# Linear attention feeding a gated two-layer network: joint token tails, loads held back and a second queue at the start

## The chip, the cores and the metric

The kernel runs on one core of a Trainium2 chip. The metric is device time in microseconds (us), the median of several executions; a trace of one execution per kernel gives the details, and its span is about 1.75 us shorter than the device time. The kernel before takes 296.5 us.

## The reference, cut to what matters

```python
# attention without softmax, 8 batches x 8 heads x 576 tokens x 64
q_p, k_p = phi(q), phi(k)               # phi(x) = min(exp(x), max(x, 0) + 1)
kv  = einsum('bhsd,bhse->bhde', k_p, v)
z   = sum(k_p, axis=2)
num = einsum('bhsd,bhde->bhse', q_p, kv)
den = einsum('bhsd,bhd->bhs', q_p, z) + 1e-6
x   = (num / den)                       # as [8*576 tokens, 512]
h   = x @ w_in                          # 512 -> 2048
g   = h / (1 + exp(-beta * h))
out = g @ w_out                         # 2048 -> 512
```

The 576 tokens of a batch are four tiles of 128 and a tail of 64. The eight tails are collected in `xT_tail` and go through the network last, as a ninth batch.

## The kernel before

The program is ordered by hand. Each batch has an input phase (`h_phase`, 64 matmuls of 512 columns and their silu on ScalarE, ACT) and an output phase (`y_phase`, 64 matmuls). The attention of the next batch is woven into them through `plan`: what to run after which matmul group. The parts that the change and the argument touch, with cuts marked `# ...`:

```python
def num_mm(b, t):                       # numerator and denominator of one token tile
    n = rows(t)                         # 128, or 64 for the tail
    # ...
    for p in range(KC):
        nc.tensor.matmul(nps[:n, p // 2, c0 : c0 + 2 * (D + 1)],
                         st[b, "qT"][:, t, p, :n], kv_bd[b % 2][p // 2][:, p % 2], ...)

# start: q, k, v and the weights all on GpSimd's queue; q, k, v and w_in are cast to bf16 on the way
load_nine(k9, k); load_nine(q9, q, j1=4); # ... v, rest of q, w_in, w_out, k and q of batch 1

# output phase of batch 0
load_next(2)                            # k, q, v of batch 2, behind v of batch 1 and the last of w_out
# ...
w_out_scale(2); phi(1, 1); v_copy(1); phi(1, 0)
y_phase_wide(0, {
    4: [F(load_next, 3)],
    9: [F(kv_mm, 1), F(kv_evac, 1), F(w_out_scale, 3)],
    10: [F(q_trans, 1, 0, 1, wide=True), F(q_trans, 1, 2, 3, wide=True)],
    11: [F(num_mm, 1, 0), F(num_norm, 1, 0)],
    # ...
})
# input phase of batch 1:  12: [F(v_copy, 2), F(load_next, 4)]
# output phase of batch 1: 1: [F(phi, 2, 0), F(q_trans_dma, 2), F(phi, 2, 1)]  (q of batch 2, by DMA)
```

Of the kernel before, what the change touches and what calls it, by code (L numbers as in the profile page):

```python
# [11 lines left out]
ALU = mybir.AluOpType  # L12
# [4 lines left out]
def kernel(  # L17
# [99 lines left out]
    def nine(a, spec):  # L117

        names = " ".join(spec)
        flat = a.rearrange("p a b c -> p (a b c)")  # L120
        size = {"h": HH, "j": N9, "d": D}
        n = size["h"] * size["j"] * size["d"]
        return flat[:, 0:n].rearrange(f"p ({names}) -> p {names}", **size)

    q9 = nine(xqk[0][:, 0], "hjd")
    k9 = nine(xqk[0][:, 1], "hjd")
    v9 = nine(vraw[0], "hjd")

    def load_nine(dst, src, h0=0, h1=HH, j0=0, j1=N9):
        for g in range(2):  # L130
            nc.gpsimd.dma_start(  # L131
                out=dst[g * TAIL : (g + 1) * TAIL, h0:h1, j0:j1, :].rearrange(
                    "p h j d -> p h (j d)"
                ),
                in_=src[0, g * HH + h0 : g * HH + h1, :, :]
                .rearrange("h (p j) d -> p h j d", j=N9)[:, :, j0:j1, :]
                .rearrange("p h j d -> p h (j d)"),
            )
# [4 lines left out]
    nc.vector.memset(g_sb[0][:, FC - 1, :], 0.0)  # L143
    clear_tail(1)
    nc.vector.memset(vraw[1][TAIL:P, :, NJ, :], 0.0)
    beta_row = consts.tile([FC, P], F32)
    nc.sync.dma_start(out=beta_row, in_=moe_beta.rearrange("(c p) -> c p", p=P))
# [3 lines left out]
    load_nine(k9, k)  # L151
    load_nine(q9, q, j1=4)
    make_identity(nc, identity)
    make_identity(nc, ident16)
    load_nine(v9, v, j1=6)
    load_nine(v9, v, j0=6)
    load_nine(q9, q, j0=4)
    for i in range(4):
# [9 lines left out]
    kv_bd = [  # L168
        [consts.tile([P, 2, 2, D + 1], BF16, name=f"kv_bd{i}{g}") for g in range(2)]
        for i in range(2)  # L170
    ]
    for i in range(2):
        for g in range(2):
            nc.vector.memset(kv_bd[i][g], 0.0)
# [32 lines left out]
    def w_out_scale(i, dve=True):  # L207
        for c in range(4):
            ff = 4 * i + c
            dst, src, by = w_out_sb[i][:, c, :], w_out_f[i][c // 2][:, c % 2, :], rbeta[:, ff : ff + 1]  # L210
            if dve:
                nc.vector.tensor_scalar(dst, src, by, None, ALU.mult)
            else:
                nc.scalar.activation(dst, src, ACTF.Copy, scale=by)
# [33 lines left out]
    x0 = {0: q9, 1: k9}  # L248
# [4 lines left out]
    def exp0(a, j0, j1):  # L253
        if j0 == 0:
            st["e0", a] = work9("e", bufs=3)
        nc.scalar.activation(  # L256
            st["e0", a][:, j0:j1].rearrange("p j h d -> p h j d"), x0[a][:, :, j0:j1],
            ACTF.Exp,
        )

    def relu0(a, j0, j1):
        if j0 == 0:
            st["r0", a] = work9("r")
        nc.vector.tensor_scalar(
            st["r0", a][:, j0:j1].rearrange("p j h d -> p h j d"), x0[a][:, :, j0:j1],
            0.0, 1.0, ALU.max, ALU.add,
        )

    def phi0(a, j0, j1):
        nc.vector.tensor_tensor(  # L270
            st["p0"][a][:, j0:j1], st["r0", a][:, j0:j1], st["e0", a][:, j0:j1], ALU.min
        )

    def q_trans0(t, banks, c0):


        for jj in range(2 if t < NJ else 1):
            for a in range(2):
                for g in range(2):
                    gs = slice(g * TAIL, (g + 1) * TAIL)  # L280
                    m0 = c0 + a * P + jj * TAIL
                    nc.tensor.matmul(
                        banks[:, g, m0 : m0 + TAIL],
                        st["p0"][0][gs, 2 * t + jj, 2 * a : 2 * a + 2, :],
                        identity[gs, gs],
                        is_transpose=True, start=True, stop=True, skip_group_check=True,
                    )

    def q_out0(t, banks, c0, dve):
        n = rows(t)  # L290
        src = banks[:, :, c0 : c0 + 2 * P].rearrange("p g (a n) -> p g a n", a=2)
        dst = st[0, "qT"][:, t].rearrange("p (g a) n -> p g a n", g=2)
        copy(dst[:, :, :, :n], src[:, :, :, :n], dve)
# [5 lines left out]
    def kv_mm0(kvp, j0, j1, of_v):  # L299


        for j in range(j0, j1):
            for a in range(2):
                for g in range(2):
# [4 lines left out]
                        st["p0"][1][gs, j, 2 * a : 2 * a + 2, :],  # L309
# [6 lines left out]
    def kv_evac0(kvp):  # L316
        for g in range(2):
            for i in range(2):
                gs = slice(i * D, (i + 1) * D)
                copy(  # L320
                    kv_bd[0][g][gs, :, i, :],
                    kvp[g][gs, 0 : 4 * (D + 1)].rearrange(
                        "p (a i e) -> p a i e", a=2, i=2
                    )[:, :, i, :],
                    g == 0,
                )
# [24 lines left out]
    def kv_evac(b):  # L351
        for i in range(2):
            for g in range(2):
                gs = slice(g * D, (g + 1) * D)
                nc.vector.tensor_copy(  # L355
                    kv_bd[b % 2][i][gs, :, g, :], st[b, "kvp"][gs, 2 * i : 2 * i + 2, :]
                )
# [16 lines left out]
    def q_trans(b, *ts, wide=False, dve=False):  # L374

        n, m = rows(ts[0]), len(ts)
        tp = tr_bank(wide).rearrange("p (t c n) -> p t c n", t=2, c=KC)
# [7 lines left out]
        copy(st[b, "qT"][:, ts[0] : ts[0] + m, :, :n], tp[:, 0:m, :, :n], dve)  # L385
# [7 lines left out]
    def num_mm(b, t):  # L393
        n = rows(t)
        nps = att_banks()
        st[b, "n", t] = nps
        for p in range(KC):
            c0 = (p % 2) * 2 * (D + 1)
            nc.tensor.matmul(  # L399
                nps[:n, p // 2, c0 : c0 + 2 * (D + 1)],  # L400
                st[b, "qT"][:, t, p, :n],
                kv_bd[b % 2][p // 2][:, p % 2],
                start=True, stop=True, skip_group_check=True,
            )

    def num_norm(b, t):
        n = rows(t)
# [10 lines left out]
        if by_dma(b):  # L418
# [4 lines left out]
    def x_dst(b, t):  # L423
        if t < NJ:
            return xT[b % 3][:, t]
        return xT_tail[:, :, b * TAIL : (b + 1) * TAIL]

    def x_trans(b, t, wide=False, dve=False):
        n = rows(t)
# [51 lines left out]
    out0 = out[0:S, :].rearrange("(p j) m -> p j m", j=N9)  # L481

    def tail_rows(b):
        if b == 0:
            return out0[:, N9 - 1, :]
        return out[b * S + MAIN : (b + 1) * S, :]

    def store(b, t, y_sb):
        if b < B:
            if b == 0:  # L490
                for i in range(2):
                    nc.sync.dma_start(
                        out=out0[:, 2 * t + i, :], in_=y_sb[i * TAIL : (i + 1) * TAIL, :]
# [68 lines left out]

    def load_next(b):
        if b < B:
# [4 lines left out]
            if b < 5:  # L569
                load_v(b)  # L570

# [11 lines left out]
    def F(f, *a, **k):  # L583
        return lambda: f(*a, **k)

    begin(0)
    st["warm"] = mm_bank([P, 512])
    warm(10)
    beta_trans()
    make_beta()  # L590
    warm(20)
    st["p0"] = [
        nine(st[0, "p"][:, a].rearrange("p j (h d) -> p j h d", h=H), "jhd")
        for a in range(2)
    ]
    exp0(1, 0, 5)
    exp0(1, 5, N9)
    exp0(0, 0, 4)
    relu0(1, 0, 5)
    relu0(1, 5, N9)  # L600
    phi0(1, 0, 5)
    relu0(0, 0, 4)
    phi0(1, 5, N9)
    phi0(0, 0, 4)
    kvp = [mm_bank([P, 512]) for _ in range(2)]
    kv_mm0(kvp, 0, N9, False)
    qb = att_banks(BF16)
    q_trans0(0, qb, 0)
    q_trans0(1, qb, 256)
    q_out0(0, qb, 0, False)  # L610
    q_out0(1, qb, 256, False)
    kv_mm0(kvp, 0, 6, True)
    kv_mm0(kvp, 6, N9, True)
    kv_evac0(kvp)
# [4 lines left out]
    exp0(0, 4, N9)  # L619
    relu0(0, 4, N9)  # L620
    silu_table()
    num_norm(0, 0)
    phi0(0, 4, 6)
    warm(4)
    x_trans(0, 0, dve=True)
    qb2 = att_banks(BF16)
    q_trans0(2, qb2, 0)
    q_out0(2, qb2, 0, False)
    num_norm(0, 1)
    phi0(0, 6, N9)  # L630
# [6 lines left out]
    def tidy0():  # L637
# [3 lines left out]
    def q_rest0():  # L641
        q_trans0(3, qb2, 256)
        q_trans0(4, qb2, 512)
        q_out0(3, qb2, 256, False)
        q_out0(4, qb2, 512, False)
# [7 lines left out]
            3: [F(x_trans, 0, 1), F(num_mm, 0, 2), F(num_norm, 0, 2), F(q_rest0)],  # L653
            5: [F(num_mm, 0, 3), F(num_norm, 0, 3)],
            7: [F(x_trans, 0, 2)],
            8: [F(num_mm, 0, 4), F(num_norm, 0, 4)],
            9: [F(x_trans, 0, 3), F(tidy0)],
            12: [F(x_trans, 0, 4)],
# [5 lines left out]
    clear_tail(2)  # L664
    load_next(2)
# [9 lines left out]
    v_copy(1)  # L675
    phi(1, 0)
    y_phase_wide(0, {
        4: [F(load_next, 3)],
        9: [F(kv_mm, 1), F(kv_evac, 1), F(w_out_scale, 3)],
        10: [F(q_trans, 1, 0, 1, wide=True), F(q_trans, 1, 2, 3, wide=True)],  # L680
# [3 lines left out]
        14: [F(num_mm, 1, 3), F(num_norm, 1, 3), F(q_trans, 1, 4, wide=True)],  # L684
# [9 lines left out]
            3: [F(x_trans, 1, 4)],  # L694
            8: [F(begin, 2), F(relu, 2, 0)],
            10: [F(relu, 2, 1)],
            12: [F(v_copy, 2), F(load_next, 4)],
# [9 lines left out]
        6: [F(kv_mm, 2), F(kv_evac, 2)],  # L707
        11: [F(num_mm, 2, 0), F(num_norm, 2, 0)],
        12: [F(num_mm, 2, 1), F(num_norm, 2, 1), F(x_trans, 2, 0, wide=True)],
        13: [F(num_mm, 2, 2), F(num_norm, 2, 2), F(x_trans, 2, 1, wide=True)],  # L710
        14: [F(num_mm, 2, 3), F(num_norm, 2, 3)],
    })

    for b in range(2, B + 1):
# [3 lines left out]
        if b == 2:  # L718
# [4 lines left out]
                0: [F(x_trans, 2, 2), F(num_mm, 2, 4), F(num_norm, 2, 4)],  # L723
                1: [F(x_trans, 2, 3)],
                3: [F(x_trans, 2, 4)],
# [15 lines left out]
        if n < B:  # L741
            for t in range(NT):
# [33 lines left out]
```

## Time and profile before

The profile names engines PE (TensorE matmul), PEld (weight load), DVE (VectorE), ACT (ScalarE), POOL (GpSimd) and SP (SyncE). In the trace I take the first matmul of each phase as its beginning. That cuts the span into pieces that can be compared between kernels:

| piece | from us | length us |
|---|---|---|
| start, to the first real matmul | 0 | 17.16 |
| input phase of batch 0 | 17.16 | 17.00 |
| output phase of batch 0 | 34.16 | 18.37 |
| input phase of batch 1 | 52.53 | 15.08 |
| output phase of batch 1 | 67.61 | 17.64 |
| input phase of batch 2 | 85.25 | 15.94 |
| output phase of batch 2 and all later ones | 101.19 | 193.91 |

### The profile page before, as it was taken

To read this page: it belongs to the slowest core of one execution; us is meant where nothing else is said; L and a number is where in the kernel's file an instruction comes from. 1 tells how busy PE (TensorE), PEld (TensorE's weight loads), DVE (VectorE), ACT (ScalarE), POOL (GpSimd) and SP (SyncE) were. 2 spreads that over 40 slices of the span, in tenths; PEclk is the share of its full clock that TensorE was granted. 3 is DMA by queue.
4 is the path that set the end of the run, shared out by engine and by line. 5 is a ranking of instruction groups with operands and counts; after the bars stand their busy time and mean duration, and the time that the engine had idled before them with its cause. 6 is when DMAs were issued, how large, how long until landed. Compare 5 with 4: busy or idle time off the path is not lost.

```text
span 295.1 us, 4750 instructions
## 1 busy us (share of the span) xinstructions
PE 283.9 (96%) x1891; PEld 143.9 (49%) x1912; DVE 124.0 (42%) x261; ACT 175.1 (59%) x234; POOL 52.7 (18%) x72
## 2 busy tenths in 40 slices
PE   8879999999999999999999999999999999999994
PEld 3557445644465544445444544454445444444444
DVE  4765488504365174616461646154715400110012
ACT  2788786889988780778087907790770077018500
POOL 8924474540003200330023000000000000000000
PEclk9999999999999999999999999999999999999999
DMA  7999999999637993699369945024502400120032
GB/s 103 196 207 343 256 272 192 256 193 192 89 142 100 175 131 113 130 174 154 98 129 159 159 109 124 2 71 116 127 0 72 118 36 0 38 90 16 0 73 71
DMA packets 72310, 37.09 MB, mean 126 GB/s; under 512 B 40912, under 2 KB 66784, under 8 KB 72288
## 3 DMA queue, kind: packets, MB, share of 16 engines
q0 software_dynamic: 38912, 20.45, 47.9%
q1 hardware_dynamic: 33216, 16.20, 22.9%
q8 instruction: 15, 0.25, 0.3%
q10 hardware_dynamic: 160, 0.13, 0.2%
q14 instruction: 7, 0.06, 0.1%
HBM read 36.71 MB, written 9.44 MB: 156 GB/s over the span
## 4 chain that ended last, share of the span: by engine, by line
PE 76%; DMA 9%; POOL 4%; ACT 4%; issue 4%; DVE 1%; ACTq 0%; POOLq 0%; DVEq 0%
PE mm L453 37%; PE mm L505 33%; DMA xT<-in_moe_w_out_dram 5%; DMA vraw<-in_v_dram 4%; PE att L399 3%; ACT e L229 2%; POOL xqk L131 1%; PE att L344 1%; PE mm L537 1%; POOL w_in L159 1%; ACT L229 1%; POOL vraw L131 1%; ACT g L445 1%; DVE qk_p L242 0%; POOL xqk L111 0%
## 5 line engine op out<-in xcount | busy, mean ns | idle before, releaser
L445 ACT ACTIVATE g<-mm,beta_c 128x512 bf16<-128x512 f32 (+2 forms) x156 | 97.3, 633 | 88.4 <-PE mm L453 88.1
L505 PE MATMUL mm<-w_out,g 128*128 128x512 bf16 x541 | 126.7, 379 | 1.2 <-issue 0.3
L453 PE MATMUL mm<-xT,w_in 128*128 128x512 bf16 (+2 forms) x560 | 108.1, 349 | 1.4 <-DMA w_in<-in_moe_w_in_dram 1.1
L453 PEld LDWEIGHTS <-w_in 128*128 128x128 bf16 x656 | 61.9, 98 | 62.4 <-DMA w_in<-in_moe_w_in_dram 1.2
L505 PEld LDWEIGHTS <-g 128*128 128x128 bf16 x560 | 53.0, 98 | 58.2
L515 DVE COPY y_sb<-mm 128x512 f32<-128x512 f32 x27 | 18.7, 691 | 70.6 <-PE mm L505 69.1
L229 ACT ACTIVATE e<-xqk 128x2560 bf16<-128x2560 bf16 x14 | 31.9, 2329 | 0.1
L415 DVE TENSOR_TENSOR xs<-att,rden 128x512 bf16<-128x512 f32 (+1 forms) x40 | 27.6, 689 | 1.4
L242 DVE TENSOR_TENSOR qk_p<-r,e 128x2560 bf16<-128x2560 bf16 x14 | 20.9, 1490 | 13.1 <-ACT e L229 12.4
L355 DVE CAST kv_bd<-att 64x130 bf16<-64x130 f32 x28 | 8.2, 292 | 32.2 <-PE att L344 31.8
L72 POOL DMA_DIRECT2D vraw<-in_v_dram x7 | 6.4, 909 | 84.2 <-DVE vaug L370 78.5
L413 DVE TENSOR_SCALAR den<-att 128x8 f32<-128x8 f32 (+1 forms) x40 | 6.5, 161 | 32.0 <-PE att L399 31.9
L399 PE MATMUL att<-kv_bd,q_pT 128*128 128x130 bf16 (+1 forms) x160 | 15.8, 221 | 1.1 <-DVE kv_bd L370 0.7
L399 PEld LDWEIGHTS <-q_pT 128*128 128x128 bf16 (+1 forms) x160 | 11.6, 100 | 10.7 <-DVE xs L415 2.4
L453 PE MATMUL mm<-xT_tail,w_in 128*128 128x512 bf16 x63 | 13.9, 379 | 0.1
L237 DVE TENSOR_SCALAR r<-xqk 128x2560 bf16<-128x2560 bf16 x14 | 11.6, 834 | 3.8 <-DMA xqk<-in_q_dram 2.3
L575 PE MATMUL mm<-g 128*128 128x512 bf16 x34 | 9.9, 452 | 1.2 <-DVE g L143 1.2
L229 ACT ACT_TABLE_LOAD x7 | 9.0, 1283 | 0.1
L414 DVE RECIPROCAL rden<-den 128x8 f32<-128x8 f32 (+1 forms) x40 | 8.1, 202 | 1.4
L72 POOL DMA_DIRECT2D xqk<-in_k_dram x7 | 6.9, 984 | 6.3 <-DMA w_in<-in_moe_w_in_dram 2.8
L76 POOL DMA_DIRECT2D xqk<-in_k_dram x7 | 7.4, 1057 | 1.5 <-DMA w_in<-in_moe_w_in_dram 1.3
L256 ACT ACTIVATE e<-xqk 128x1280 bf16<-128x1280 bf16 (+1 forms) x4 | 4.4, 1155 | 5.4 <-DMA xqk<-in_k_dram 5.3
(71 smaller groups left out, 140.0 us busy)
## 6 DMA issues: line engine op xcount, KB each, us to landing
out_dram<-y_sb SPq DMA_DIRECT2D x28, 256.0 KB, 2.3
xqk<-in_k_dram POOLq DMA_DIRECT2D x7, 512.0 KB, 10.7
xqk<-in_q_dram POOLq DMA_DIRECT2D x7, 512.0 KB, 11.3
vraw<-in_v_dram POOLq DMA_DIRECT2D x7, 512.0 KB, 11.3
w_in<-in_moe_w_in_dram POOLq DMA_DIRECT2D x4, 512.0 KB, 11.0
g<-in_moe_w_out_dram POOLq DMA_DIRECT2D x4, 512.0 KB, 10.9
out_dram<-y_sb SPq DMA_DIRECT2D x14, 128.0 KB, 5.2
xqk<-in_moe_w_out_dram POOLq DMA_DIRECT2D x2, 512.0 KB, 14.4
```

The lines of the kernel that those rows point to most:

```text
L72: eng.dma_start(out=dst[:, :, 0:NJ, :].rearrange("p h j d -> p h (j d)"), in_=src[b, :, 0:MAIN, :].rearrange("h (p j) d -> p h (j d)", j=NJ),)
L229: nc.scalar.activation(st[b, "e", a][:, h0:h1], xqk[b % NX][:, a, h0:h1], ACTF.Exp)
L237: nc.vector.tensor_scalar(st[b, "r", a][:, h0:h1], xqk[b % NX][:, a, h0:h1], 0.0, 1.0, ALU.max, ALU.add)
L242: nc.vector.tensor_tensor(st[b, "p"][:, a].rearrange("p j (h d) -> p h j d", h=H)[:, h0:h1], st[b, "r", a][:, h0:h1], st[b, "e", a][:, h0: ...
L355: nc.vector.tensor_copy(kv_bd[b % 2][i][gs, :, g, :], st[b, "kvp"][gs, 2 * i : 2 * i + 2, :])
L399: nc.tensor.matmul(nps[:n, p // 2, c0 : c0 + 2 * (D + 1)], st[b, "qT"][:, t, p, :n], kv_bd[b % 2][p // 2][:, p % 2], start=True, stop=True ...
L415: nc.vector.tensor_mul(xs[:n], nv[:, :, :, 0:D], rden[:n, :, :, None].to_broadcast([n, 2, 4, D]))
L445: nc.scalar.activation(g_sb[b % 2][:, ff, c0:c1], hp[:, c0:c1], ACTF.Silu, scale=beta_c[:, ff : ff + 1],)
L453: nc.tensor.matmul(hp[:, c0:c1], w_in_sb[ff // 4][:, kc, (ff % 4) * P : (ff % 4 + 1) * P], x[:, t0:t1, kc, :] if b < B else x[:, kc, c0:c1 ...
L505: nc.tensor.matmul(yp, g_sb[b % 2][:, ff, t * P : (t + 1) * P], w_out_sb[ff // 4][:, ff % 4, :], start=(ff == 0), stop=(ff == FC - 1),)
L515: nc.vector.tensor_copy(y_sb, yp)
L575: nc.tensor.matmul(st["warm"], g_sb[0][:, FC - 1, 0:P], g_sb[0][:, FC - 1, :], start=True, stop=True, skip_group_check=True,)
```

## The change

Its intent, as its author put it: joint tails; batch 4's loads behind q of batch 2; batch 2's loads held until v of batch 1 has landed. The diff also moves part of k to SP's queue and reorders the first phases. Its core:

```diff
+    k_last = g_f[...]                                  # float32 staging for 4/9 of k of batch 0
+    load_nine(k_last, k, KF, N9, eng=nc.sync)          # KF = 5, N9 = 9
-    load_nine(k9, k)
+    load_nine(x9[1][:, :, 0:KF], k, 0, KF)
     # num_mm: the tails of batches b-1 and b (b odd) into rows 0..63 and 64..127 of one bank
+            for i in range(1 if t < NJ else 2):
+                bb, n, r0 = (b, P, 0) if t < NJ else (b - 1 + i, TAIL, i * TAIL)
     # num_norm: the joint tail's x is transposed by DMA in every batch
-        if by_dma(b):
+        if by_dma(b) or t == NJ:
     # kv_evac: two copies of 260 columns for four of 130
     # loads
+    hold(vraw[1][0:1, 0, NT - 1, 0:1])                 # GpSimd reads one element: waits for v of batch 1
     load_next(2)
+    def held_load(b, n):
+        hold(st[n, "qT"][0:1, NJ, KC - 1, 0:1])        # waits for the transposed q of batch n
+        load_next(b)
     # warm-up matmuls ahead of the first kv: 10 + 20 become 10 + 15
     # output phase of batch 0
-    v_copy(1)
+    v_copy(1, 0, HH); v_copy(1, HH, H, dve=False)
-        9: [F(kv_mm, 1), F(kv_evac, 1), F(w_out_scale, 3)],
-        10: [F(q_trans, 1, 0, 1, wide=True), F(q_trans, 1, 2, 3, wide=True)],
+        10: [F(q_trans, 1, 0, 1, 2, 3), F(kv_mm, 1), F(kv_evac, 1), F(w_out_scale, 3, 2)],
     # input phase of batch 1
-            12: [F(v_copy, 2), F(load_next, 4)],
+            12: [F(v_copy, 2)],
     # output phase of batch 1: batch 4's loads behind q; x of batch 2 copied by DVE
-        6: [F(kv_mm, 2), F(kv_evac, 2)],
+        6: [F(kv_mm, 2), F(kv_evac, 2), F(held_load, 4, 2)],
-        12: [..., F(x_trans, 2, 0, wide=True)],
+        12: [..., F(x_trans, 2, 0, wide=True, dve=True)],
     # batches 2 to 7: tails only with the odd batch
-            for t in range(NT):
+            for t in range(NT if n % 2 else NJ):
     # cut: renamed helpers, order of the first q transposes and copies, beta on ACT's queue
```

## The prediction

> **What bounds the kernel now.** I read the page first. TensorE (PE) is busy 96% of the span, nearly everywhere at a granted clock of nine tenths or more (1.00 in every stretch I asked for).
>
> ```profile
> span 295.1 us, 4750 instructions
> PE 283.9 (96%) x1891; PEld 143.9 (49%) x1912; DVE 124.0 (42%) x261; ACT 175.1 (59%) x234; POOL 52.7 (18%) x72
> ...
> PE   8879999999999999999999999999999999999994
> DMA  7999999999637993699369945024502400120032
> ```
>
> The reader is to see two things. PE is the bound from about the third slice to the end, so only three kinds of saving count: PE work removed, PE waits removed, and an earlier start of the real work. And DMA is full for the first quarter, so whatever PE waits for there is decided by the order of the bytes.
>
> I then split the time with the chain of waits in order of time. One regular batch is 29.87 us (116.54 to 146.41): 64 input matmuls, 64 output matmuls (52 in 11.22 us, so 0.216 us each, 13.8 us a phase), 40 small kv matmuls (0.75 us) and five groups of four numerator matmuls:
>
> ```profile
> 116.54 11.22 PE mm L453 x52
> 127.77 0.75 PE att L344 x40
> 128.52 2.70 PE mm L453 x12
> ...
> 138.81 0.23 PE att L399 x4
> ...
> 140.77 0.35 PE att L399 x4
> ```
>
> The reader is to see that a group for a full 128-token tile takes 0.23 us, while the last one, for the 64-token tail, takes 0.35 us: half the rows cost more. Nothing else is slack in this stretch, so batches 3 to 8 offer only tails.
>
> The rest is at the front. Waits of PE up to 54 us, and the table of stretches for the output phase of batch 1:
>
> ```profile
> PE mm L453 <- DMA w_in<-in_moe_w_in_dram: 1.1, 1, 1.1
> PE att L399 <- DVE kv_bd L370: 0.7, 1, 0.7
> ...
> 67.80:85.25 17.45, 16.11 (x125) 8.04 (x127) 7.90 (x18) 16.80 (x17) 0.00 (x0) 1.00 0.88 134
> ```
>
> First line: the first real matmul starts at 17.16 us and waits for the first quarter of w_in, although its x was ready at 16.3. Last line (length, busy time of PE, weight loads, DVE, ACT, POOL, then clock, DMA share, GB/s): PE idles 1.34 us while ACT is busy 16.80 of 17.45. Two named waits there:
>
> ```profile
> PE att L433 <- ACT xT L372: 0.6, 1, 0.6
> PE att L399 <- DMA q_pT<-qk_p: 0.3, 1, 0.3
> ```
>
> The output phase of batch 0 (34.3 to 52.5) is the third place: PE busy 17.25 of 18.20. The chain runs there over the landing of v of batch 1 at 41.8, the last phi (43.10 to 44.57), four kv evictions (1.2 us) and only then the second half of the q transposes at 45.75.
>
> **What the Trainium skill says.** "TensorEngine Tiling (Array Packing)", Key Properties: changing the tiling mode drains the array, and different tiles run in parallel. The trace agrees with both: the 64-column tail group costs 0.12 us more than a full one, and the 40 kv matmuls, which alternate between two column halves, take 0.75 us, 19 ns each, less than the 27 ns that 65 columns would take at 0.216 us per 512. "DMA: Bandwidth & Descriptors", Issuing engines are not separate DMA queues: all issuers share the same 16 engines, so a second issuer saves only issue time. The trace agrees: the sum of shares is above 1 from 3 us on whichever queue is used, but 0.03 and 0.39 in the second and third microsecond, when GpSimd is still issuing. The same page, SWDGE vs HWDGE: a cast in flight needs GpSimd; that is why the part of k moved to the SP queue lands as float32. "TensorE: Matmul & The Clock Gate", Part 1: the array starts at half rate and about 3.4 us of activity release it. The trace agrees: ten warm-ups take 4.43 us, the next twenty 4.49.
>
> **The change part by part.**
>
> *Joint tails.* Numerators of two batches' tails go into one 128-row bank. Eight tail groups of four (0.35 us each, 2.8 us) become four groups of eight that alternate column halves. At one drain each and two halves in parallel I put a group at 0.40 us (0.35 plus a little for four more loads): 1.6 us. Saved: 1.2 us of PE, all of it on the path. The three PE transposes of tails (batches 0, 1, 2; 0.22 us each in the chain) go to the DMA and are needed only at 263 us: 0.66 us. Four tail normalisations on DVE go (1.05 us each), beside the path. Sum **1.9 us**.
>
> *The start.* Four ninths of k (0.52 MB) are issued by SP at 0.75 us instead of GpSimd at 1.25 to 2.6. GpSimd's issue count stays, so its later issues don't move earlier. What moves is the bytes: the queue ahead of w_in loses 0.26 MB as written in bf16, 1.3 us at the 200 GB/s of these microseconds, and its replacement can run in part in the emptier time before 3 us. Landings of the first k should come 1.0 to 1.5 us earlier (7.49 before), and with them exp, phi, kv and x. w_in lands about 1 us earlier. The author takes away five of the thirty warm-ups, 1.1 us of PE, which fits. I take **1.0 us**, the smaller of the two chains.
>
> *First input phase.* The q transposes, copies and numerators are reordered; one transposition group moves in from idle time (0.2 us) and some small waits go (0.3 us listed for ACT xT). Net **0.1 us**.
>
> *Output phase of batch 0.* Four q transposes in one go without waiting for the kv bank, two kv evictions instead of four (about 0.45 each instead of 0.29), v copied half on DVE and half on ACT. PE's needs here sum to 13.8 + 0.75 + 1.2 + 0.9 + 0.44 = 17.1 of 18.2 us, so at most 1.1 can be won. Against it: the ACT half of the v copy waits behind the table load, and half of the last w_out scaling goes to ACT. I take **0.6 us**. The hold of batch 2's loads I count as nothing by itself: v of batch 1 landed 11.6 us after issue, k and q of batch 2 were issued after it, and landings follow issue order, so they hardly delay it.
>
> *Output phase of batch 1.* Batch 4's loads no longer stand ahead of the transposition of q of batch 2 (9.0 us at its longest, 5.3 median), and x is copied by DVE, not by the ACT that has 16.80 us to do. Needs: 13.8 + 0.75 + 0.92 + 0.44 = 15.9 of 17.45 us, so at most 1.5. I take **1.2 us**. The delayed loads of batch 4 (about 10 us) are first read after 100 us, and issued near 75: hidden.
>
> Sum: 1.9 + 1.0 + 0.1 + 0.6 + 1.2 = 4.8 us. 296.4 - 4.8 = 291.6; I say **291.5**.
>
> **The rivals.** (1) *w_in still gates the start.* If the SP part of k is spread over the same full engines, w_in lands where it did and the earlier x waits for it: the start gives 0.3 at most, and 292.3. For it: share above 1 from 3 us. Against it: the empty second and third microsecond. (2) *ACT takes the place of the loads in the output phases.* In batch 0's phase exp, table loads, half of v, two q copies and two w_out scalings stand in one queue; if the v copy or the last scaling comes late, kv or the matmuls of the last w_out quarter stop, and the 0.6 becomes zero or a loss of 0.5: 292 to 292.7. For it: the phase before it already ends on 8.60 busy of 9.04 us for ACT. (3) *The holds matter more than I think.* If engines interleave the loads, v of batch 1 comes 2 us sooner, the phase gives its full 1.1 and every bubble of batch 1's goes too: 290 and the verdict tips. Against it: landings in order of issue. (4) *DMA transposes of the joint tails or the late loads collide with output stores.* They have tens of microseconds of room; up to 0.3 us.
>
> **Range and chances.** 2% faster is under 290.5, one microsecond below my value. Rivals 1 and 2 pull upwards by 0.7 to 1.2 us each, rival 3 and small bubbles that I haven't named pull down by about 1.5. So 289.3 to 294.0 eight times in ten. Faster by over 2%: 0.32; within 2%: 0.66; slower: 0.02, since PE work is removed and nothing is added to it.
>
> **What would show it.** In the changed kernel: four numerator groups of eight at 0.35 to 0.45 us, no PE transposes into the joint tail; the first exp near 6.2 us and the first real matmul near 16.1, still listed as waiting for w_in; the output phase of batch 0 close to 17.5 us long, with kv before 44 us; the output phase of batch 1 close to 16.2, its two named waits gone and q's transposition near 5 us; regular batches at 29.87 and 29.5 in turn. The prediction is wrong if the first matmul doesn't move, if a joint tail group takes 0.6 us (its halves then run one after the other), or if PE stops in either output phase for an ACT copy.

## The result, and the profile after

The changed kernel takes 293.32 us (293.01 to 294.14, four executions) against 296.46. Ratios here are the mean time of one kernel's runs over that of the other's runs of the same rounds, so not quite the ratio of the medians; this one is 0.9898, interval 0.9876 to 0.9919. So 1.0% faster, 3.1 us of the 4.9 forecast, and within the range. A second series of the same kernel gave 293.74 and 0.9905.

The head of its page, with PE's line by slices and DMA's:

```profile
span 291.4 us, 4695 instructions
PE 280.9 (96%) x1875; PEld 142.5 (49%) x1895; DVE 118.8 (41%) x239; ACT 173.3 (59%) x228; POOL 51.0 (18%) x74
...
PE   8879998999999999999999999999999999999994
DMA  8999999999899986797379755032503400120033
```

PE's busy time fell by 3.0 us and its share stayed at 96%. About 1.0 us of that is the five warm-up matmuls (9.9 us for 34 before, 8.9 for 29 now), which fill a wait at the start; so about 2.0 of the 3.7 us won in the span is PE work of the program that is no longer done. Pieces as before:

| piece | before us | changed us | difference | forecast |
|---|---|---|---|---|
| start | 17.16 | 16.87 | -0.29 | -1.0 |
| input phase of batch 0 | 17.00 | 16.27 | -0.73 | -0.1 and a tail |
| output phase of batch 0 | 18.37 | 18.51 | +0.14 | -0.6 |
| input phase of batch 1 | 15.08 | 14.88 | -0.20 | a tail |
| output phase of batch 1 | 17.64 | 16.67 | -0.97 | -1.2 |
| input phase of batch 2 | 15.94 | 15.16 | -0.78 | a tail |
| the rest | 193.91 | 193.04 | -0.87 | two tails |

They sum to -3.70, the difference of the spans. They come from one trace of each kernel, and the first three move from trace to trace: the nine traces in this document whose program is the same up to the first real matmul have it between 15.67 and 17.48 us. The other four agree to 0.02 us in the changed kernel's two traces. What PE waited for in the changed kernel (in total, times, longest, in us; for the kernel before see the prediction):

```profile
PE mm L475 <- DMA w_in<-in_moe_w_in_dram: 1.7, 1, 1.7
...
PE att L421 <- DVE kv_bd L385: 0.4, 1, 0.4
...
PE att L421 <- ACT q_pT L387: 0.3, 1, 0.3
PE mm L527 <- DVE w_out L212: 0.3, 1, 0.3
```

The two waits named for the output phase of batch 1 are no longer listed. The wait for w_in grew from 1.1 to 1.7: x was ready earlier (15.6 us, not 16.3), w_in hardly. And the output phase of batch 0 has two new waits. One is for ACT's copy of q (the line of PE's timeline below, with the idle time and its releaser in brackets), the other for w_out on DVE:

```profile
45.72 0.40 PE L421 MATMUL att<-kv_bd,q_pT 128*128 128x130 bf16 x4 [0.31 <-ACT q_pT L387]
```

The chain of waits for that phase (start, length, what):

```profile
42.80 0.89 PE att L395 x16
43.69 0.77 PE att L362 x40
44.46 0.02 issue
44.48 0.42 DVE kv_bd L372
...
44.92 0.43 DVE kv_bd L372
45.35 0.03 issue
45.38 1.19 DVE w_out L212 x2
46.58 0.03 issue
46.61 0.18 DVE den L435
```

Sixteen q transposes and forty kv matmuls (L362) now run without a gap, but then DVE does three things in a row: two evictions, two scalings of w_out, and only then the first normalisation, for which PE waits. The last line of batch 0's phase moved from 52.53 to 51.65 only because it began 1.02 us earlier.

Joint tails, in the chain of waits of the output phase of batch 2:

```profile
107.06 1.03 PE mm L527 x4
108.09 0.36 PE att L421 x8
```

Eight matmuls take 0.36 us, where four took 0.35.

### The profile page after: what moved, and what is told of

Same layout as the page of the kernel before. It is cut to its first block, busy times and chain, and to the rows that moved or that the text cites. A ratio compares the mean times of both kernels' runs of the same rounds, so it can differ in the third digit from the quotient of the medians.

```text
span 291.4 us, 4695 instructions
## 1 busy us (share of the span) xinstructions
PE 280.9 (96%) x1875; PEld 142.5 (49%) x1895; DVE 118.8 (41%) x239; ACT 173.3 (59%) x228; POOL 51.0 (18%) x74
## 4 chain that ended last, share of the span: by engine, by line
PE 90%; DMA 3%; POOL 2%; DVE 2%; issue 1%; POOLq 0%
PE mm L475 41%; PE mm L527 40%; DMA w_in<-in_moe_w_in_dram 3%; PE att L421 3%; PE att L475 2%; PE att L362 2%; POOL xqk L135 1%; PE mm L559 1%; POOL vraw L135 1%; DVE xs L437 1%; PE mm L455 1%; DVE w_out L212 0%; PE att L395 0%; PE att L455 0%; DVE kv_bd L372 0%
## 5 line engine op out<-in xcount | busy, mean ns | idle before, releaser
L437 DVE TENSOR_TENSOR xs<-att,rden 128x512 bf16<-128x512 f32 x36 | 24.9, 692 | 1.2
L372 DVE CAST kv_bd<-att 64x260 bf16<-64x260 f32 x14 | 6.0, 427 | 33.4 <-PE att L362 33.3
L435 DVE TENSOR_SCALAR den<-att 128x8 f32<-128x8 f32 x36 | 5.9, 163 | 29.5 <-PE att L421 29.4
L421 PEld LDWEIGHTS <-q_pT 128*128 128x128 bf16 (+1 forms) x160 | 10.7, 100 | 9.5 <-DVE xs L437 1.9
L421 PE MATMUL att<-kv_bd,q_pT 128*128 128x130 bf16 (+1 forms) x160 | 14.2, 222 | 0.8 <-DVE kv_bd L385 0.4
L237 DVE TENSOR_SCALAR r<-xqk 128x2560 bf16<-128x2560 bf16 x14 | 11.6, 831 | 4.0 <-DMA xqk<-in_q_dram 2.5
L608 PE MATMUL mm<-g 128*128 128x512 bf16 x29 | 8.9, 463 | 1.3 <-DVE g L145 1.2
L436 DVE RECIPROCAL rden<-den 128x8 f32<-128x8 f32 x36 | 7.3, 203 | 1.2
L475 PE MATMUL att<-xT,w_in 128*128 128x512 bf16 x32 | 7.2, 379 | 0.0
L385 DVE COPY vaug<-vraw 128x2560 bf16<-128x2560 bf16 (+1 forms) x7 | 5.4, 774 | 3.5 <-DMA vraw<-in_v_dram 3.5
L72 POOL DMA_DIRECT2D xqk<-in_k_dram x7 | 6.3, 900 | 2.9 <-DMA w_in<-in_moe_w_in_dram 2.9
## 6 DMA issues: line engine op xcount, KB each, us to landing
vraw<-in_v_dram POOLq DMA_DIRECT2D x7, 512.0 KB, 12.2
```

What stands on the lines that cost most here:

```text
L72: eng.dma_start(out=dst[:, :, 0:NJ, :].rearrange("p h j d -> p h (j d)"), in_=src[b, :, 0:MAIN, :].rearrange("h (p j) d -> p h (j d)", j=NJ),)
L237: nc.vector.tensor_scalar(st[b, "r", a][:, h0:h1], xqk[b % NX][:, a, h0:h1], 0.0, 1.0, ALU.max, ALU.add)
L421: nc.tensor.matmul(nps[r0 : r0 + n, p // 2, c0 : c0 + 2 * (D + 1)], st[bb, "qT"][:, t, p, :n], kv_bd[bb % 2][:, p], start=True, stop=True, ...
L436: nc.vector.reciprocal(rden[:n], den[:n])
L437: nc.vector.tensor_mul(xs[:n], nv[:, :, :, 0:D], rden[:n, :, :, None].to_broadcast([n, 2, 4, D]))
L475: nc.tensor.matmul(hp[:, c0:c1], w_in_sb[ff // 4][:, kc, (ff % 4) * P : (ff % 4 + 1) * P], x[:, t0:t1, kc, :] if b < B else x[:, kc, c0:c1 ...
```

## The experiments

Each is the changed kernel with one edit, unless said otherwise. Line numbers shift a little from kernel to kernel.

### Tails apart again

```diff
-            for i in range(1 if t < NJ else 2):
-                bb, n, r0 = (b, P, 0) if t < NJ else (b - 1 + i, TAIL, i * TAIL)
+            for i in range(1):
+                bb, n, r0 = b, rows(t), 0      # and one tail a batch in all the plans
```

> The changed kernel with only the joint tails undone: every batch's tail has its own four numerator matmuls and its own normalisation, and the tails of batches 0 to 2 are transposed on PE again. Theory (tails are most of what was gained): +2.1 us on the changed kernel's 293.3, so 295.4: four groups of about 0.45 us come back (1.8) and three PE transposes of 0.22 (0.66), less some of it hidden in the output phase of batch 0. Rival (the gain is from the loads and the reordering, tails were hidden): +0.5 or less, 293.8.

Measured: 296.03 us (295.43 to 296.48), ratio 0.9974 (0.9951 to 0.9997) to the kernel before. By pieces, against the trace of the changed kernel's second series (whose start was of the same kind): input phases of batches 0, 1 and 2 +0.26, +0.21 and +0.79, the output phase of batch 2 and all later +0.80. Sum 2.1 us; the medians say 2.3 to 2.7. The tails are two thirds of the gain, as the theory had it. The pieces can't simply be added to those of other runs: in the input phase of batch 2 the tail gives 0.79 here and the copies by DVE give 0.30 in a run below, yet the change as a whole gave 0.78 there.

### k on one queue

```diff
-    load_nine(k_last, k, KF, N9, eng=nc.sync)
-    load_nine(x9[1][:, :, 0:KF], k, 0, KF)
+    load_nine(x9[1], k, 0, N9)
```

> The changed kernel with the whole of k loaded by GpSimd in its cast form, nothing by SP. Theory (the 16 engines are full from 3 us on, so a second issuer moves no bytes sooner; w_in gates the first real matmul): first real matmul 0.2 to 0.4 us later than 16.87, time +0.3 or less. Rival (what I predicted: the second queue brings k and w_in 1 us sooner): +1.0. A second rival: without the float32 copy w_in comes as soon or sooner, and x is still ready first: 0.0 or a small gain.

Measured: 293.73 us, ratio 0.9905 (0.9876 to 0.9934), the same as the changed kernel's 0.9898 and 0.9905. The wait for w_in in its trace:

```profile
PE mm L472 <- DMA w_in<-in_moe_w_in_dram: 1.8, 1, 1.8
```

The first real matmul comes at 16.70 us, not later but 0.17 sooner, so the second queue is worth nothing that these runs can see. The first exp, which waits for k, begins at 7.16 us here; it began at 7.44 in the changed kernel, at 7.49 before, and at 7.14 or later in every trace with the second queue. The second queue did move bytes earlier: 106, 273 and 242 GB/s in the three microseconds from 2 to 5 us, against 36, 173 and 188 here, which is 0.22 MB more. But SP's part of k is 0.52 MB as float32 and would be 0.26 as bf16, so by this estimate nearly all of the gain goes into the wider type. This agrees with "DMA: Bandwidth & Descriptors" in the Trainium skill, Issuing engines are not separate DMA queues: a second issuer saves only the time to issue. One trace can't settle less than about a microsecond, though. In the nine traces with the changed kernel's start the quickest of w_in's four transfers took 7.0 to 8.7 us from issue to landing, with the same bytes in the queues, and I don't know why. Where it took 8.4 us or more, PE waited for w_in; at 7.0 to 7.2 it waited for x.

### w_in ahead of the rest of q

```diff
-    load_nine(x9[0][:, :, QF:N9], q, QF, N9)
     for i in range(4):
         nc.gpsimd.dma_start(out=w_in_sb[i], ...)
+        if i == 0:
+            load_nine(x9[0][:, :, QF:N9], q, QF, N9)
```

> The changed kernel with the first quarter of w_in ahead of the last five ninths of q of batch 0 on GpSimd's queue, 0.65 MB less ahead of it. Theory (bytes ahead of w_in gate the first real matmul): it starts 1.2 us sooner, at 15.7, where x bounds it; but exp of the rest of q comes 2.4 us later and the silu table after it, so silu starts near 18 and the phase ends no sooner: time 293.3 within 0.5. Rival (w_in lands when its own issue lets it): first real matmul stays at 16.8.

Measured: 295.88 us, ratio 0.9981 (0.9955 to 1.0007): slower than the changed kernel by 2.1 to 2.6 us. This is a miss by 2.6 us. PE no longer waits for w_in. But that doesn't show that the bytes ahead of it decide when it lands: w_in was also issued 1.2 us sooner (7.09 us, not 8.29), and it landed 6.9 us after issue, against 7.1 in the second series of the changed kernel with those bytes ahead of it. And x is not ready at 15.7, as I had expected it to be:

```profile
PE mm L476 <- DVE xT L386: 2.8, 1, 2.8
```

In DVE's program the copy of the first x stands behind the relu of the rest of q, and the trace has them in this order:

```profile
16.77 0.49 DVE L275 TENSOR_SCALAR r<-xqk 128x1280 bf16<-128x1280 bf16 x1 [2.46 <-DMA xqk<-in_q_dram]
17.18 0.42 DVE L386 COPY xT<-mm 128x512 bf16<-128x512 bf16 x1
```

DVE idles 2.46 us for that part of q, which comes later here, so the first real matmul starts at 17.65 us and silu later still. What is taken from one transfer at the start is paid by the next.

### Batch 4's loads where they were

```diff
-        6: [F(kv_mm, 2), F(kv_evac, 2), F(held_load, 4, 2)],
+        6: [F(kv_mm, 2), F(kv_evac, 2)],
-            12: [F(v_copy, 2)],
+            12: [F(v_copy, 2), F(load_next, 4)],
```

> The changed kernel with batch 4's loads issued where they were before, ahead of the transposition of q of batch 2. Theory (the hold is worth what PE waited for q): the transposition goes from 3.1 us issue to landing near 9, PE waits 0.3 to 0.8 us in the output phase of batch 1, +0.5 us, 293.8. Rival 1 (the x copies moved from ACT to DVE are the whole gain there): +0.0. Rival 2 (the loads delay more than q, for example v of batch 3): +1.0 or more.

Measured: 301.45 us, ratio 1.0154 (1.0130 to 1.0179): 8 us slower than the changed kernel and 5 slower than the kernel before, which has its loads in this very place. Only the "+1.0 or more" of rival 2 covers that, and the wait is the one for q that the first theory named, at 4.9 us and not 0.3 to 0.8. PE's longest wait, and then the table of stretches (length, busy time and instructions of PE, PEld, DVE, ACT and POOL, granted clock, DMA share, GB/s):

```profile
PE att L421 <- DMA q_pT<-qk_p: 4.9, 1, 4.9
```

```profile
84.00:88.00 4.00, 3.52 (x18) 2.12 (x19) 1.72 (x6) 0.60 (x1) 0.00 (x0) 0.50 0.00 0
88.00:92.00 4.00, 3.81 (x27) 2.13 (x27) 3.18 (x9) 1.41 (x3) 0.00 (x0) 0.93 0.43 166
```

The transposition of q of batch 2, issued at 70.89 us, landed 13.5 us later, and PE stood still for 4.9 us. During the wait the clock of PE fell: it was 0.50 between 84 and 88 us and 0.93 in the next four. The output phase of batch 1 took 23.37 us instead of 16.67. So the second hold doesn't win 0.5 us: it keeps 6.7 us in this phase from being lost. (Of the rest of the 8, this trace has 1.4 in the input phase of batch 0, where its clock was 0.50 from 17 to 20 us, long before the edit.) The next runs asked what had made the place unsafe.

### Neither hold

```diff
-    hold(vraw[1][0:1, 0, NT - 1, 0:1])
     load_next(2)
     # and batch 4's loads as in the run before
```

> The changed kernel with neither hold: batch 2's loads not held for v of batch 1, batch 4's loads issued where they were before. Theory (the hold of batch 2 pushes all later loads back by 2 to 3 us, so that batch 4's collide with the transposition of q of batch 2; the second hold mends what the first broke): q's transposition lands near 79 as in the kernel before, PE waits 0.3 to 0.8 us for it, and the time is 293.3 to 294.0, some 8 us below the run with the first hold alone. Rival (batch 4's loads by themselves collide with the transposition in the changed kernel's order): near 301.

Measured: 298.53 us (297.1 to 299.86), ratio 1.0061 (1.0037 to 1.0086). The theory that the first hold had pushed the loads back holds for 2.9 us, by which this run is faster than the one before (q lands at 81.6 us, not 84.4). It falls for the larger part: without the hold q's transposition still lands 12.5 us after issue, and PE waits 3.9 us. The rival's number, 301, is missed too, and it doesn't say what in the changed order makes the loads collide, since the kernel before had the same loads in the same place and landed q at 79.3. The issue of q's transposition with its us to landing, in this run and in the kernel before, and PE's wait in this run:

```profile
q_pT<-qk_p SPq DMA_TRANSPOSE x1, 12.5
```

```profile
q_pT<-qk_p SPq DMA_TRANSPOSE x1, 9.0
```

```profile
PE att L421 <- DMA q_pT<-qk_p: 3.9, 1, 3.9
```

The trace shows something else, a fall of the transfer rate while loads are waiting (last two columns: DMA share and GB/s):

```profile
58.00:59.00 1.00, 1.00 (x6) 0.49 (x5) 0.00 (x0) 0.81 (x2) 0.00 (x0) 1.00 1.50 192
59.00:60.00 1.00, 1.00 (x7) 0.42 (x5) 0.00 (x0) 0.82 (x2) 0.00 (x0) 1.00 2.35 78
60.00:61.00 1.00, 1.00 (x6) 0.47 (x5) 0.00 (x0) 0.82 (x2) 0.23 (x1) 1.00 0.89 112
```

What is in flight there is the transposition of the first joint tail, which the change moved from PE to the DMA. It was issued at 53.98 us and took 8.2 us to land; the other three joint tails took 3.0 to 4.3. In the kernel before, at 59 to 61 us, the rate was 197 and 186 GB/s.

### Neither hold, first joint tail transposed by PE

```diff
-            if by_dma(b) or t == NJ:
+            if by_dma(b) or (t == NJ and b != 1):
     # input phase of batch 1, with both holds away
+            3: [F(x_trans, 1, 4)],
```

> The changed kernel with neither hold and with the first joint tail (batches 0 and 1) transposed by four PE matmuls and an ACT copy, not by the DMA. Theory (that one DMA transposition, issued at 54 us into full queues, landed 8.2 us later and cost the loads about 2 us near 59 to 61 us; this pushed batch 4's loads onto the transposition of q of batch 2): no dip of the transfer rate near 60 us, q's transposition lands near 79 as in the kernel before, PE waits under 1 us for it, time 293.3 to 294.3, some 4 us below the run with neither hold (298.5). Rival (the loads of batch 4 collide with q's transposition because the changed kernel reaches that point 1 us sooner): lands near 81, time 297.5 or more.

Measured: 294.56 us (294.08 to 295.01), ratio 0.9931 (0.9916 to 0.9945): 4.0 us below the run before. The same two microseconds:

```profile
59.00:60.00 1.00, 1.00 (x7) 0.41 (x6) 0.00 (x0) 0.82 (x2) 1.00 (x2) 1.00 1.42 200
60.00:61.00 1.00, 1.00 (x6) 0.48 (x5) 0.00 (x0) 0.82 (x2) 0.21 (x1) 1.00 1.78 179
```

No dip, and q's transposition takes 8.4 us:

```profile
q_pT<-qk_p SPq DMA_TRANSPOSE x1, 8.4
```

It lands at 78.4 us, PE has no wait for it above the smallest that is listed (0.2 us), and the output phase of batch 1 takes 16.68 us, as short as with both holds. So one part of the change (the tail by DMA) made the collision, and another (the hold of batch 4's loads) took it away. That the dip alone accounts for the whole shift of q isn't shown: GpSimd issued q of batch 4 2.1 us later in the run with the dip (60.77 us, not 58.65), and q's own transposition ran beside loads for longer there. The remaining microsecond to 293.5 I can't place wholly: this run's mean clocks were low in five of six executions (0.986 to 0.994), and in its trace the clock was 0.50 from 18 to 20 us, which made the input phase of batch 0 17.35 us long.

### Batch 2's loads without their hold

```diff
-    hold(vraw[1][0:1, 0, NT - 1, 0:1])
     load_next(2)
```

> The changed kernel without the hold of batch 2's loads. Theory (landings follow the order of issue, so loads issued after v of batch 1 can't delay it): v of batch 1 lands at 41.7 as in both kernels, time 293.3 within 0.2. Rival (the hold gives v its bandwidth): v lands 1 us or more later, time +0.5 or more.

Measured: 292.93 us, ratio 0.9876 (0.9853 to 0.9900), a little below the changed kernel's 0.9898 and 0.9905 with overlapping intervals. The two parts of v of batch 1 landed 12.2 and 11.5 us after their issue here, 12.2 and 11.6 in the changed kernel. So k and q of batch 2, issued from 36.88 us on while v was still under way on the same queue of GpSimd, didn't delay v, and the hold earns nothing. (It isn't a rule for all queues: the tail's transposition on SP's queue, above, did slow loads that had been issued before it.)

The traces even point to a price of the hold. With it GpSimd issues the loads of batches 2 and 3 from 42.2 us on, and the two scalings of w_out on DVE, which PE waits for, took 1.19 to 1.59 us in seven traces and 0.98 in an eighth; in the three traces without it that scale at the same place they took 0.88, as here:

```profile
46.27 0.88 DVE L212 TENSOR_SCALAR w_out<-g,rbeta 128x512 bf16<-128x512 f32 x2
```

The stretch from the first q transposition to the end of the output phase of batch 0 takes 9.02 and 9.41 us in the changed kernel's two traces, and 8.70 to 8.71 in these three. Why the scalings are slower there isn't shown; in these three traces GpSimd issues little or nothing while DVE scales.

The trace of this run happens to show something else, from 11 to 16 us (columns as above, the clock being third from the right):

```profile
11.00:12.00 1.00, 0.83 (x40) 0.68 (x34) 0.96 (x5) 0.34 (x2) 1.00 (x2) 0.86 1.37 198
12.00:13.00 1.00, 0.96 (x22) 0.96 (x22) 0.83 (x4) 0.41 (x1) 1.00 (x2) 0.50 1.30 190
...
14.00:15.00 1.00, 0.87 (x7) 0.57 (x6) 0.64 (x3) 1.00 (x2) 0.65 (x1) 0.50 1.24 205
15.00:16.00 1.00, 0.84 (x7) 0.48 (x6) 0.82 (x2) 0.98 (x2) 0.00 (x0) 0.93 1.23 212
```

The granted clock falls to half for 3 us, soon after the warm-up. Its mean over the execution is 0.994 then. Of 33 executions of the kernel before in these series 5 had a mean below 0.996; of 10 of the changed kernel 7 had, and those took 293.9 us on average, the other three 293.1.

### More warm-ups

```diff
-    warm(15)
+    warm(20)
     x_trans(0, 0, dve=True)
+    warm(6)
     num_norm(0, 1)
```

> The changed kernel with 20 warm-up matmuls and not 15 ahead of kv, and 6 more in the wait for w_in. Theory (the shorter warm-up leaves PE idle long enough that in about half of the executions the granted clock falls to 0.5 for some 3 us, which costs about 1 us): all runs at clock 1.0, median 293.0, the runs within 0.3 us of each other. Rival (the clock falls for another reason): clocks of 0.993 remain. If the extra warm-ups stand in the way of kv: first real matmul later than 16.9.

Measured: 293.68 us, ratio 0.9893 (0.9876 to 0.9910). The clock part came out as expected, four of four executions at 0.998 or above, but four don't settle it: the run of the next section, which keeps the 15 warm-ups, had five of six at 0.997 or above. The time part doesn't hold: no gain. In the trace the output phase of batch 0 took 19.61 us, because the second half of the third quarter of w_out had landed only by 39.2 us (by 38.5 in the changed kernel's trace), and DVE does the phi of batch 1 only after scaling it. So the fall of the clock is there, its cost (0.9 us, from the two groups of executions) is a correlation, and neither that the missing warm-ups cause it nor that more of them buy the time back is shown.

### x of batch 2 copied by ACT

```diff
-        12: [..., F(x_trans, 2, 0, wide=True, dve=True)],
+        12: [..., F(x_trans, 2, 0, wide=True)],
     # and three more copies alike
```

> The changed kernel with x of batch 2 copied by ACT again and not by DVE (four copies, two in the output phase of batch 1, two in the input phase of batch 2). Theory (the wait of 0.6 us for ACT's copy returns, because ACT is 16.8 of 17.5 us busy there): +0.5 to 0.7, 293.9. Rival (the hold of batch 4's loads alone made that phase shorter): +0.1 or less.

Measured: 293.69 us, ratio 0.9911 (0.9889 to 0.9932), against 293.74 and 0.9905 in the same rounds: by the medians, no difference. By pieces, the output phase of batch 1 is 16.93 us (16.67 with DVE) and the input phase of batch 2 15.46 (15.16): 0.56 us, as expected. The medians hide it, because five of six executions had a clock of 0.997 or above here and one of six of the changed kernel in these rounds. Over both series the executions at 0.997 or above give 293.7 us here (mean of five) and 293.1 for the changed kernel (three): 0.6. PE's wait is back:

```profile
PE att L455 <- ACT xT L387: 0.3, 1, 0.3
```

### The scaling ahead of the evictions

```diff
-            F(q_trans, 1, 0, 1, 2, 3), F(kv_mm, 1), F(kv_evac, 1), F(w_out_scale, 3, 2),
+            F(q_trans, 1, 0, 1, 2, 3), F(w_out_scale, 3, 2, 0, 2), F(kv_mm, 1),
+            F(kv_evac, 1), F(w_out_scale, 3, 2, 2, 4),      # chunks 0, 1 (DVE) and 2, 3 (ACT)
```

> The changed kernel with DVE's half of the last w_out scaling placed ahead of the two kv evictions, in DVE's idle 1.9 us, and not behind them. Theory (in the output phase of batch 0 PE waits for DVE's order: scaling 1.19 us, then the first normalisation): the first PE transpose of x of batch 1 comes about 1 us sooner, 0.7 to 1.1 us gained, 292.4. Rival (the landing of v of batch 1 or of the last w_out bounds this phase): the scaling waits for its data, the evictions are pushed back, 0.0 or a loss.

Measured: 292.87 us (292.18 to 293.12), ratio 0.9868 (0.9851 to 0.9884), the lowest ratio of all. DVE in order of time (start, length, line, operation, idle before):

```profile
42.60 0.89 DVE L212 TENSOR_SCALAR w_out<-g,rbeta 128x512 bf16<-128x512 f32 x2 [0.21 <-DMA g<-in_moe_w_out_dram]
43.91 0.87 DVE L372 CAST kv_bd<-att 64x260 bf16<-64x260 f32 x2 [0.42 <-PE att L362]
45.58 0.17 DVE L435 TENSOR_SCALAR den<-att 128x8 f32<-128x8 f32 x1 [0.80 <-PE att L421]
```

The scaling is done before the evictions want DVE, and the first normalisation starts at 45.58 us, not 46.61. The output phase of batch 0 takes 18.18 us instead of 18.51 (18.91 in the second series). From the first q transposition to its end it is 8.66 us, 0.4 to 0.8 less than in the changed kernel. But without the hold of batch 2's loads, and with the scaling left in place, it was nearly as short (8.70). Moving the scaling may thus mostly repair what the hold costs. It is less than the 0.7 to 1.1 of the theory: the next wait is close behind, for ACT, which copies q until 45.1 us and then scales the other half of w_out (0.2 us of PE waiting).

### Put together

The edits of the last section, of batch 2's hold, and 18 warm-ups for 15.

> A version put together from what the runs show: the changed kernel with DVE's half of the last w_out scaling ahead of the kv evictions, without the hold of batch 2's loads, and with 18 warm-ups for 15. Theory: 0.5 to 0.8 us below the changed kernel in the same rounds, 292.4, with fewer executions at a granted clock below 0.997. Rival (the three are within noise together, because the landings of v of batch 1 and of the last w_out bound that phase): no difference beyond 0.2.

Measured: 292.94 us, ratio 0.9880 (0.9862 to 0.9898), the changed kernel in the same rounds 293.74 and 0.9905 (0.9885 to 0.9925). Four of five executions had a clock of 0.997 or above. Lower by 0.3%, with overlapping intervals, and not better than the scaling alone. That fits: the scaling ahead and the hold taken away win the same microseconds, 8.67 us here from the first q transposition to the end of the phase.

### The changed kernel once more

> The changed kernel as it is, for comparison in the same rounds: 293.3, executions at clock 1.0 near 293.0 and those at 0.993 near 294.0.

Measured: 293.74 us (293.01 to 294.50), the first real matmul at 16.66 us in its trace; five of six clocks from 0.992 to 0.994.

## Why the prediction was right, point by point

- **What bounds the kernel.** Right: PE is at 96% before and after, and the batches from 3 on gave little but tails: 0.87 us in 193, of which 0.80 went with the tails when they were undone.
- **Joint tails, 1.9 us.** Right in mechanism and nearly in size: a group of eight takes 0.36 us (I had said 0.40), and undoing the tails costs 2.1 us by pieces. The step that failed is inside it: that the tails' transposes "go to the DMA and are needed only at 263 us" took them as free. The first one lay for 8.2 us in full queues, the rate fell to 78 and 112 GB/s, and without either hold that cost PE 3.9 us of waiting. My fourth rival looked for a collision with output stores, at most 0.3 us; it came with the loads. That the hold of batch 4's loads kept this cost out of the total was luck for the forecast: I had counted that hold as a gain and not seen what it guarded against.
- **The start, 1.0 us.** Not borne out: 0.29 in the profiled runs, where w_in gates the start, as rival 1 had it. The step that failed is that the second queue lands the first k 1.0 to 1.5 us earlier: the first exp was to come near 6.2 us and came at 7.44, and never before 7.14. I had taken the time before 3 us as free capacity, and the third microsecond took 0.07 MB more; and I had counted what leaves GpSimd's queue (0.26 MB) more than what comes in its place (0.52). Whether w_in or x gates differs from trace to trace (15.67 to 17.48 us for the first real matmul), so that one trace doesn't give the size. I also took the five warm-ups that were cut as evidence that the author had gained that time. Executions with a low clock were more frequent afterwards (7 of 10 against 5 of 33); that the cut caused it isn't shown.
- **First input phase, 0.1 us besides its tail.** Too small: it is 0.73 us shorter, of which the tail explains 0.26. But start and phase trade with each other (the phase is 16.27 us long in the changed kernel's first trace, where w_in gates the start, and 16.86 in its second, where x does), so only their sum counts: 1.02 us in the profiled run, where I had 1.1 and a tail's 0.57.
- **Output phase of batch 0, 0.6 us.** Wrong: no gain, +0.14 in the first trace and +0.54 in the second. Rival 2 had the kind right, an engine's order taking the place of the landing of v. Its engine, ACT, is one part: PE stops 0.31 us for ACT's copy of q. That is the last of the signs of being wrong that I had named. DVE is the other: PE stops 0.3 us for the scaling of w_out, which also stands ahead of the first normalisation. Moving that scaling, or taking the hold of batch 2 away, gave back 0.3 to 0.8. An upper limit got from PE's needs alone says nothing of the order on the engines that feed it.
- **Output phase of batch 1, 1.2 us.** Nearly right in size, 0.97; in mechanism shown only in part. The copies by DVE are 0.26 of it here, and 0.30 more in the next phase. That batch 4's loads stand behind q gives the rest is not shown: with these loads ahead of q and the first joint tail on PE the phase was just as short (16.68 us). The order of the x transposes changed there too, and no run undid that alone. That the held loads of batch 4 would be hidden held.
- **The hold of batch 2's loads counts as nothing.** Right for the landing of v, so rival 3 is out; but the output phase of batch 0 was 0.3 to 0.7 us shorter behind the first q transposition without it.
- **The other signs.** Groups of eight at 0.36 us (0.35 to 0.45 forecast), kv matmuls at 43.69 us (before 44), q's transposition in 4.8 us (near 5) and regular batches at 29.42 and 29.88 us in turn (29.5 and 29.87) came as said. The first real matmul at 16.87 us (16.1) and the output phases of 18.51 us (17.5) and 16.67 us (16.2) did not.

So the sum of 4.8 became 3.1 to 3.7: the start and the output phase of batch 0 together gave 0.15 where I had 1.6, and the tails and the first input phase gave a little more than forecast.

## What to carry to other kernels

Work moved from the bounding engine to the DMA wasn't free here while the queues were full: look at what is in flight at the moment of the new transfer, and at who waits next for something behind it. A hold on a load may be the repair of another part of the same change, so undo parts together as well as singly. And when two queues share the same full engines, or a wait ends, look for the next thing in line (here the order on DVE and ACT) before counting a gain.

## What the Trainium skill lacked or had wrong

- "DMA: Bandwidth & Descriptors", Rules for kernel authors: a transpose beside ordinary transfers needs nothing, it says, which is about correctness. No page gives the cost beside full queues: one 128x512 bf16 transposition took 8.2 us to land there (3.0 to 4.3 us for the three later ones of the same trace), and the rate fell from 192 to 78 and 112 GB/s for two microseconds; with PE doing it the rate was 200 and 179.
- "TensorE: Matmul & The Clock Gate", Part 1, gives idle stretches of over about 3.4 us as what throttles the clock again, and also tells of a kernel with frequent short idles whose clock went to and fro. Here it fell to 0.50 for 3 us at the start in an execution whose longest single PE wait there was 1.2 us, between matmuls of 2 to 128 columns; that is nearer to the second account, but which of these counts as idle no run here settles.
- The same page, Part 1, gives about 25 ns as the least time from one matmul to the next. That was lower here: the 40 kv matmuls, which alternate between two column halves, take 0.75 us, 19 ns each.
- "TensorEngine Tiling (Array Packing)", Key Properties, says that a change of the tiling mode drains the array, and gives no time for it. Four numerator matmuls of 64 columns between others of 128 took 0.35 us and four of 128 columns 0.23; no run separates a drain from other causes of these 0.12 us. That different tiles run in parallel is borne out: eight tail matmuls on two column halves take 0.36 us.
